# An attention loop whose two lanes run one score product apart, written two units to a body, with each small piece in a body of its own

## The chip, the core and the metric

The kernel runs on one core of a Trainium2 chip. The metric is the device time of one execution in microseconds (us): the median of several executions. An execution that the hardware profiler records gives the trace; times "in the trace" are counted from the start of its span.

## What is computed

Inputs are float32: q, k, v of 4 batches x 8 heads x 768 tokens x 64, 16 centroids for each head, and the matrices of a token mixing that follows. The reference, cut to its core:

```python
q_assign = np.argmax(np.einsum('bhsd,hcd->bhsc', q_n, c_n), axis=-1)
k_assign = np.argmax(np.einsum('bhsd,hcd->bhsc', k_n, c_n), axis=-1)
mask = q_assign[:, :, :, None] == k_assign[:, :, None, :]
scores = scale * np.matmul(q, k.transpose(0, 1, 3, 2))
scores = np.where(mask, scores, -1000000000.0)
scores = scores - np.max(scores, axis=-1, keepdims=True)
attn = np.exp(scores)
attn = attn / (np.sum(attn, axis=-1, keepdims=True) + 1e-09)
x = np.matmul(attn, v)                    # then (batch, token, 512)
...
theta = x @ w_theta
zr, zi = x * np.cos(theta), x * np.sin(theta)
y = np.einsum('ts,bsd->btd', w_tok_r, zr) + np.einsum('ts,bsd->btd', w_tok_i, zi)
u = x + y
return u + np.maximum(u @ w_ch, 0.0)
```

Every token goes to its nearest centroid, a query sees only the keys of its own cluster, and the result passes through a rotation, a mixing over the tokens and a small layer over the channels. The change touches the first part, the attention.

## The kernel before

**Tiling.** The 32 heads are taken in 16 pairs (`pi`). The two heads of a pair are the two lanes (`j`): lane 0 holds its 64 channels in partitions 0 to 63, lane 1 in 64 to 127. A matmul of one lane uses 64 rows of TensorE, and matmuls of both lanes that are next to each other in the program run at the same time. A pair is worked off in 12 units (`u`): 2 halves of the queries (`a`, 384 wide) by 6 blocks of 128 keys (`i`). There are 192 units (`NUT`), and one pass of the main loop (L784) is a body of two units, so a pair has six bodies.

**One unit.** Float32 values are kept as a rounded part and a rest (`hq`, `lq`, `hk`, `lk`). The scores of a lane are four matmuls into one PSUM bank (`score_products`, L455): hk with hq, hk with lq, lk with hq, and mk with mq. The last adds the mask: `mq` has a one at the row of the query's cluster and the negative maximum in row 32 of each lane, `mk` has a large negative number wherever a key is not in that cluster. ScalarE then exponentiates the bank (`exps`, L471), GpSimd adds the exponentials of three blocks to each other (`add_exps`, L482), VectorE adds the two sums that this leaves (`add_sums`, L486), and TensorE multiplies the exponentials by v (`weighted`, L543, the tile `av`). The maximum over the keys has to be known first. So in each body TensorE also computes, for a block of queries ten units ahead (`LEAD`), four products of each lane into a tile `m` of two banks (`max_products`, L410), which VectorE reduces (`max_of`, L430).

**PSUM.** There are two tiles of two banks (`m_tile`), three single banks (`bank`), and one bank for `av`. The score tiles `sc` and all small tiles take the three single banks in turn.

**Small pieces.** Besides its units, every pair needs on the way, two pairs ahead: its rows of q and k loaded (`load_raw`), their rounded parts (L390, L394), the centroid products `lg` (`logits`, L286, four matmuls), their transposition `lt` (`turn_logits`, L299, three), the maximum over 16 clusters, the comparison with it, the product with falling numbers and again the maximum (`find_max`, `first_of`: the first cluster that has the maximum, `rr`), the transposition of `rr` into `rt` (L350 or L354), its way through DRAM so that the cluster's number stands in 16 partitions (`rd`, then `clq` and `clk`, L359 and L364), and `mq` (two passes of ScalarE, L369 and L371) and `mk` (VectorE, L373) from these. For the maxima there is a transposition `mt` twice a pair (`shift_row`, L438), for the sums `sm` (L510) and their way through DRAM to `rb`, the multiply of `xt` (`normalise`), and for the second part of the kernel the unpacking of a piece of weights (`to_f32`: the operations that write `w`, and `hi`, `lo`).

**Order.** The order on each engine is that of the program; `in_order` fixes it. Tables give the unit at which a piece is written: `A_UNITS` for the ten steps of `assign`, `HI_UNITS` and `LO_UNITS` for the rounded parts, `W_UNITS` and `W_LAST` for the weights, `ADDS`, `SUMS`, `NORM` for the sums, `FIRST` for the first rotation of the second stage. `at_unit` collects them in `todo`, and `pieces(u)` writes those that are due, at three places of a body. In a body both lanes of unit u go in step; then unit u+1 of one lane at a time goes beside the m products of the other, with `av` between the two lanes:

```python
            both(score_products, u, exps)
...
            if ahead < NUT:
                scores_beside_max(u + 1, ahead, 0)
        pieces(u - 0.5)
        if 0 < u <= NUT:
            weighted(u - 2)
...
            weighted(u - 1)
...
        pieces(u)
```

When the maxima are done, ten units before the end, the m tiles take a part of the scores. SyncE issues nearly all transfers, in the order of the program.

Of the kernel before, what the change touches and what calls it, by code (L numbers as in the profile page):

```python
# [2 lines left out]

# [40 lines left out]
def kernel(  # L44
# [257 lines left out]
    def find_max(pi, ltv):  # L302
        mx = pe.tile([P, NG], F32, tag="mxl", name=f"mxl{pi}")
        nc.vector.tensor_reduce(out=mx, in_=ltv, op=ALU.max, axis=AX.X)
# [1 line left out]
        nc.vector.tensor_tensor(
            out=eq, in0=ltv, in1=mx.unsqueeze(2).broadcast_to([P, NG, C]), op=ALU.is_equal)
        return eq

    def first_of(pi, eq):  # L310
        nc.vector.tensor_tensor(out=eq, in0=eq, in1=wb, op=ALU.mult)
# [19 lines left out]
    def assign(pi):  # L331
# [15 lines left out]
        if "mt" in st.get(pi - 2, {}):  # L347
            mt = st[pi - 2].pop("mt")
            rt = mt[0:NG, P:2 * P]
            nc.tensor.transpose(out=rt, in_=rr, identity=identf)  # L350
# [11 lines left out]
        for n, x in enumerate("qk"):  # L362
            for j in range(2):
                nc.sync.dma_start(  # L364
                    out=cl[x][64 * j:64 * j + C], in_=rv[2 * n + j:2 * n + j + 1].broadcast_to([C, S]))
# [68 lines left out]
    def shift_row(pi, a):  # L434
# [5 lines left out]
        if a == 1 and 0 < pi < NPAIR - 2:  # L440

            s["mt"] = mt
        else:
            shift_out(pi, a, mt)
# [22 lines left out]
    def exps(u, j):  # L467
# [3 lines left out]
        last_exp[0] = nc.scalar.activation(out=s["at", a, i][:, j], in_=s["sc", j], func=AF.Exp, scale=SCALE)  # L471
# [627 lines left out]
```

## Time and profile before

| | |
|---|---|
| median of 3 runs | 786.07 us (784.77 to 786.43) |
| the profiled execution | 783.16 us, its span 781.4 us |
| TensorE clock granted | 1.00 |
| preparation, to the first unit | about 30 us of the span |
| attention, 16 pairs | from there to 441.8 us |
| token mixing | 441.8 us to the end |
| VectorE, ScalarE, GpSimd busy in the attention | 382.6, 265.9 and 370.7 of 411.3 us |

A time of the trace is a moment of the profiled execution or a duration; that execution was 2.9 us shorter than the median, so differences are worked out inside it. In the views a line such as `211.32 0.44 PE L408 MATMUL sc<-hq,hk` is start, length, engine, source line, operation, and the tile written with the tiles read. PE is TensorE, PEld its weight loads, DVE VectorE, ACT ScalarE, POOL GpSimd, SPq the queue of SyncE. A matmul of 384 columns is shown with 0.33 us, though the next pair of matmuls starts 0.17 us after it, since they are pipelined.

### The profile page before, as it was taken

The page shows a single profiled execution, that of the slowest core. Times are in us where ns is not written, and L with a number is a line of the kernel's source. Part 1 is how long each engine was busy: PE and PEld are TensorE (multiplying, and loading weights), DVE is VectorE, ACT ScalarE, POOL GpSimd, SP SyncE. Part 2 cuts the span into 40 slices and gives each one's busy share as a digit, 9 for nine tenths or more (in the row PEclk, how much of TensorE's full clock was granted, in tenths as well). Part 3 has the DMA queues.
Part 4 walks back from the last instruction along what each step waited for, and adds up shares of the span by engine and source line. Part 5 has one row for each costly group of instructions (what it writes and reads, how often), then busy time and mean ns, then how long its engine had stood idle before and what let it go on. Part 6 is the DMA issues. An engine that isn't in the chain of part 4 may idle for free.

```text
span 781.4 us, 14422 instructions
## 1 busy us (share of the span) xinstructions
PE 773.2 (99%) x5592; PEld 573.0 (73%) x5592; DVE 567.8 (73%) x689; ACT 388.2 (50%) x780; POOL 500.6 (64%) x289
## 2 busy tenths in 40 slices
PE   9999999999999999999999999999999999999998
PEld 6666565566666666566665588898889988899998
DVE  6789999999999999999989587844344444533322
ACT  3565757576767676767556455432333132503310
POOL 4568888989999999988987667561225112422231
PEclk9999999999999999999999999999999999999999
DMA  4113324432443244425354377124101411120001
GB/s 143 42 60 101 113 63 127 134 100 85 145 134 113 73 144 134 133 69 168 114 203 131 85 219 198 20 58 145 28 15 28 163 27 28 17 92 15 1 21 61
DMA packets 81708, 73.24 MB, mean 94 GB/s; under 512 B 59544, under 2 KB 65512, under 8 KB 81256
## 3 DMA queue, kind: packets, MB, share of 16 engines
q1 hardware_dynamic: 81634, 72.32, 31.2%
q8 instruction: 44, 0.72, 0.4%
q14 instruction: 24, 0.20, 0.1%
q10 hardware_dynamic: 6, 0.00, 0.0%
HBM read 56.89 MB, written 15.31 MB: 92 GB/s over the span
## 4 chain that ended last, share of the span: by engine, by line
PE 92%; DVE 4%; DMA 1%; issue 1%; SPq 1%; ACT 1%; POOL 0%; DVEq 0%
PE y L967 26%; PE sc L408 25%; PE av L543 15%; PE tp L643 7%; PE cy L990 5%; PE m L408 4%; PE cp L990 3%; PE lg L286 1%; PE sm L510 1%; PE y L990 1%; PE lt L299 1%; DVE acc L486 1%; DVE mk L373 1%; PE mt L438 1%; DVE nm L430 1%
## 5 line engine op out<-in xcount | busy, mean ns | idle before, releaser
L471 ACT ACTIVATE at<-sc 128x384 f32<-128x384 f32 x384 | 173.7, 495 | 97.6 <-PE m L408 57.5
L430 DVE TENSOR_REDUCE nm<-m 128x1 f32<-128x768 f32 x192 | 179.8, 946 | 21.0 <-PE m L408 19.9
L482 POOL TENSOR_TENSOR acc<-at,at 128x768 f32<-128x768 f32 x64 | 129.1, 2016 | 34.8 <-ACT at L471 34.8
L408 PE MATMUL m<-hk,hq 64*128 64x384 f32 x384 | 147.7, 385 | 0.8 <-DVE nm L430 0.6
L543 PE MATMUL av<-at,vt 128*64 128x384 f32 x768 | 145.3, 499 | 0.2 <-ACT xt L558 0.2
L918 POOL TENSOR_TENSOR zlc<-ab,zhc 128x512 fp32r<-128x512 f32 x24 | 32.9, 1371 | 162.7 <-ACT zhc L916 162.7
L482 POOL TENSOR_TENSOR acc<-acc,at 128x768 f32<-128x768 f32 x64 | 131.8, 2060 | 7.9 <-ACT at L471 5.7
L408 PE MATMUL m<-mk,mq 64*128 64x384 f32 x384 | 128.1, 334 | 0.0
L408 PE MATMUL sc<-hq,hk 64*128 64x384 f32 x384 | 117.7, 390 | 1.1 <-ACT at L471 0.9
L408 PEld LDWEIGHTS sc<-hq,hk 64*128 64x128 f32 x384 | 56.1, 183 | 61.8 <-issue 24.9
L408 PE MATMUL sc<-lq,hk 64*128 64x384 f32 x384 | 98.3, 335 | 0.0
L408 PE MATMUL sc<-mq,mk 64*128 64x384 f32 x384 | 97.8, 334 | 0.0
L408 PE MATMUL sc<-hq,lk 64*128 64x384 f32 x384 | 97.6, 333 | 0.0
L543 PEld LDWEIGHTS av<-at,vt 128*64 128x64 f32 x768 | 46.5, 136 | 58.6 <-issue 53.7
L408 PEld LDWEIGHTS m<-hk,hq 64*128 64x128 f32 x384 | 70.5, 183 | 3.3 <-DVE nm L430 2.6
L408 PEld LDWEIGHTS m<-mk,mq 64*128 64x128 f32 x384 | 71.1, 185 | 0.2 <-DVE mk L715 0.2
L649 DVE TENSOR_SCALAR kk<-tp 128x512 int32<-128x512 f32 x24 | 16.4, 685 | 73.2 <-PE tp L643 73.2
L486 DVE TENSOR_TENSOR acc<-acc,acc 128x768 f32<-128x768 f32 x30 | 69.0, 2302 | 0.0
L616 ACT CAST xh<-xT 128x512 fp32r<-128x512 f32 x23 | 14.3, 621 | 99.3 <-PE tp L643 99.3
L981 POOL TENSOR_TENSOR ul<-xT,uh 128x384 fp32r<-128x384 f32 (+1 forms) x36 | 33.5, 964 | 35.5 <-ACT uh L980 33.8
L408 PEld LDWEIGHTS sc<-mq,mk 64*128 64x128 f32 x384 | 55.3, 184 | 0.0
L408 PEld LDWEIGHTS sc<-hq,lk 64*128 64x128 f32 x384 | 55.2, 184 | 0.0
(174 smaller groups left out, 1716.3 us busy)
## 6 DMA issues: line engine op xcount, KB each, us to landing
vt<-in_v_dram SPq DMA_DIRECT2D x16, 384.0 KB
rb<-sd SPq DMA_DIRECT2D x32, 192.0 KB
xT_d<-xt SPq DMA_DIRECT2D x16, 384.0 KB
xb<-xT_d SPq DMA_DIRECT2D x96, 64.0 KB
rawq<-in_qT_dram SPq DMA_DIRECT2D x15, 384.0 KB
rawk<-in_kT_dram SPq DMA_DIRECT2D x15, 384.0 KB
w<-in_wrT_dram SPq DMA_DIRECT2D x6, 768.0 KB
xT<-xT_d SPq DMA_DIRECT2D x3, 1536.0 KB
```

What stands on the lines that cost most here:

```text
L408: nc.tensor.matmul(out, lhsT=stat[r, cols], rhs=mov[r, over], start=start, stop=stop)
L430: nc.vector.tensor_reduce(out=s["nm", a][:, j, i // 2:i // 2 + 1], in_=s["m", j][:, :, 0:HS], op=ALU.max, axis=AX.XY, negate=True)
L471: last_exp[0] = nc.scalar.activation(out=s["at", a, i][:, j], in_=s["sc", j], func=AF.Exp, scale=SCALE)
L482: last_acc[0] = nc.gpsimd.tensor_tensor(out=s["acc", a, x], in0=prev, in1=at, op=ALU.add)
L486: nc.vector.tensor_tensor(out=s["acc", a, 0], in0=s["acc", a, 0], in1=s["acc", a, 1], op=ALU.add)
L543: nc.tensor.matmul(s["av"][64 * j:64 * j + 64], lhsT=s["vt"][:, i, j, :], rhs=s["at", a, i][:, j], start=(i == 0), stop=(i == NT - 1))
L643: nc.tensor.matmul(tp, lhsT=xx[:, c, :], rhs=w_th[c][k], start=(n == 0), stop=(n == 3 * NCT - 1))
L649: nc.vector.tensor_scalar_mul(kk, tp, INV_2PI)
L918: nc.gpsimd.tensor_tensor(out=zl, in0=tr, in1=zh.bitcast(F32), op=ALU.subtract)
L967: last_mix[0] = nc.tensor.matmul(y_at(b, d, c0, c1), lhsT=zz[:, d * P:(d + 1) * P], rhs=ww[:, c0:c1], start=first and lead, stop=last, ski ...
L981: nc.gpsimd.tensor_tensor(out=ul[:, d, :], in0=x, in1=uh[:, d, :].bitcast(F32), op=ALU.subtract)
L990: nc.tensor.matmul(cp, lhsT=w_c[d][k][:, e * P:(e + 1) * P], rhs=uu[:, d, :], start=(n == 0), stop=(n == 3 * NCT - 1), skip_group_check=True)
```

## The change

**The lanes.** A body is written as one piece, after `av` and the pieces. Lane 1 is one product out of step with lane 0: where lane 0 stops a score tile, lane 1 has three of its four products done, or the other way round (`both_lanes`, and `begun` for three products that a body starts for the next one). The same matmuls are issued, in another order.

**The small pieces.** The tables are retuned: at most one of mt, lt, rt, sm and lg stands in a body, nearly always behind `av`. `lt` and `rt` take a single bank each. Before, `lt` had half of an m tile, and `rt` mostly shared the bank of a `mt`. The multiply of `xt`, the load of v, the loads of raw rows and the steps of the weights move to other units.

**The keys' mask.** `clk` is no longer one run of 768 numbers for a partition but three runs of 256 with four numbers of padding. Its loads get the same form, and so does the write of `mk`.

**The logit comparison.** `lt == maximum` is written back to PSUM in float32, and the product with the falling numbers is read from there and written as bfloat16. Before, the comparison wrote bfloat16 to SBUF, and the product read and wrote it there.

```diff
-NORM = (13, 16)
+NORM = (12, 15)
-ADDS = (8, 13)
+ADDS = (6.5, 14)
...
-    cl = {n: pe.tile([P, S], F32, name=f"cl{n}") for n in "qk"}
+    clk = pe.tile([P, 3, S // 3 + 4], F32, name="clk")
+    cl = dict(q=pe.tile([P, S], F32, name="clq"), k=clk[:, :, 0:S // 3])
...
-        lt = (m_tile(f"lt{pi}")[:, 0] if pi > 1 else bank(f"lt{pi}"))[:, 0:HS]
+        lt = bank(f"lt{pi}")[:, 0:HS]
...
+        nc.vector.tensor_tensor(
+            out=ltv, in0=ltv, in1=mx.unsqueeze(2).broadcast_to([P, NG, C]), op=ALU.is_equal)
         eq = pe.tile([P, NG, C], BF16, tag="eq", name=f"eq{pi}")
-        nc.vector.tensor_tensor(
-            out=eq, in0=ltv, in1=mx.unsqueeze(2).broadcast_to([P, NG, C]), op=ALU.is_equal)
+        nc.vector.tensor_tensor(out=eq, in0=ltv, in1=wb, op=ALU.mult)
         return eq
...
     def first_of(pi, eq):
-        nc.vector.tensor_tensor(out=eq, in0=eq, in1=wb, op=ALU.mult)
...
-        if "mt" in st.get(pi - 2, {}):
-            mt = st[pi - 2].pop("mt")
-            rt = mt[0:NG, P:2 * P]
-            nc.tensor.transpose(out=rt, in_=rr, identity=identf)
-            shift_out(pi - 2, 1, mt)
-        else:
-            rt = bank(f"rt{pi}")[0:NG, 0:P]
-            nc.tensor.transpose(out=rt, in_=rr, identity=identf)
+        rt = bank(f"rt{pi}")[0:NG, 0:P]
+        nc.tensor.transpose(out=rt, in_=rr, identity=identf)
...
+                row = rv[2 * n + j:2 * n + j + 1].broadcast_to([C, S])
                 nc.sync.dma_start(
                     out=cl[x][64 * j:64 * j + C],
+                    in_=(row if x == "q" else row.rearrange("c (a b) -> c a b", a=3)))
...
-    A_UNITS = (-9, -4, -2, -1, 2, 2, 3, 6, 7, 7.9)
+    A_UNITS = (-6, -1.5, 0, 1, 6, 6, 7, 9.5, 11.5, 10)
...
-            at_unit(u - NU + 7, load_v, pi)
+            at_unit(u - NU + 4.5, load_v, pi)
...
+    def both_lanes(p0, p1):
+
+        for x in zip_longest(p0, p1):
+            interleave(*([y] for y in x if y))
+
+    u, begun = 0, products(0, 0)
+    interleave(begun[:3])
...
+            a0, a1 = begun[3:], products(u, 1)
+            m = [max_products(ahead, j) for j in range(2)] if ahead < NUT else None
+            both_lanes(a0, a1[:1])
+            exps(u, 0)
+            if m:
+                both_lanes(m[0][:3], a1[1:])
+                exps(u, 1)
+                add_exps(u)
+                both_lanes(m[0][3:], m[1][:1])
+                max_of(ahead, 0)
+                b0 = products(u + 1, 0)
+                both_lanes(b0[:3], m[1][1:])
+                max_of(ahead, 1)
+                b1 = products(u + 1, 1)
...
+            both_lanes(b0[3:], b1[:1])
+            exps(u + 1, 0)
...
+            begun = products(u + 2, 0)
+            both_lanes(begun[:3], b1[1:])
+            exps(u + 1, 1)
             add_exps(u + 1)
```

HI_UNITS and LO_UNITS go to 3.0, 5.0 and 5.5, 7, the steps in W_UNITS move by up to 2.5 units, those in W_LAST (the last pieces of weights) by up to 11, and those in FIRST (the first rotation) by up to 1.5; the score tiles of the last bodies still take m tiles, one for each lane.

Where the instructions stand shows at three places. First TensorE, one body in the middle of the attention. In a name such as `sc86_0` 86 is the unit and 0 the lane; the number behind it counts tiles. Before:

```order
L408 MATMUL sc86_0_2999<-hq_1_145,hk_1_147 128x384
L408 MATMUL sc86_1_3000<-hq_1_145,hk_1_147 128x384
L408 MATMUL sc86_0_2999<-lq_1_146,hk_1_147 128x384
L408 MATMUL sc86_1_3000<-lq_1_146,hk_1_147 128x384
L408 MATMUL sc86_0_2999<-hq_1_145,lk_1_148 128x384
L408 MATMUL sc86_1_3000<-hq_1_145,lk_1_148 128x384
L408 MATMUL sc86_0_2999<-mq_1_149,mk_1_150 128x384
L408 MATMUL sc86_1_3000<-mq_1_149,mk_1_150 128x384
L408 MATMUL sc87_0_3013<-hq_1_145,hk_1_147 128x384
L408 MATMUL m96_1_3015<-hk_2_156,hq_2_154 128x384
```

And after the change, around the boundary of two bodies with lg (for pair 9) and lt in it:

```order
L406 MATMUL sc83_1_2927<-hq_0_163,lk_0_166 128x384
L406 MATMUL sc84_0_2932<-hq_1_145,lk_1_148 128x384
L406 MATMUL sc83_1_2927<-mq_0_167,mk_0_168 128x384
L288 MATMUL lg9_2941<-rawq9_2784,cb_188 32x384
L288 MATMUL lg9_2941<-rawk9_2786,cb_188 32x384
L288 MATMUL lg9_2941<-rawq9_2784,cb_188 32x384
L288 MATMUL lg9_2941<-rawk9_2786,cb_188 32x384
L537 MATMUL av78_2836<-at82_2880,vt6_2406 64x384 x2
L537 MATMUL av78_2836<-at83_2918,vt6_2406 64x384 x2
L301 MATMUL lt9_2956<-identf_66,lgs9_2946 128x2x4x16 x3
L406 MATMUL sc84_0_2932<-mq_1_149,mk_1_150 128x384
L406 MATMUL sc84_1_2965<-hq_1_145,hk_1_147 128x384
```

The two tiles of unit 86 stopped in one slot before; now lane 0 of unit 84 has its last product beside the first one of lane 1, and three of its products stand ahead of av. lt stands between them and takes a bank of its own.

Second VectorE, from lt to the third step of the weights (`w`, L144 to L153 before, L145 to L154 now; `acc` is L486 before and L480 now). Before:

```order
L304 TENSOR_REDUCE mxl_4345<-lt_4341 128x24
L306 TENSOR_TENSOR eq_4347<-lt_4341,mxl_4345 128x384
L430 TENSOR_REDUCE nm_4253<-m_0_4350 128x1
L311 TENSOR_TENSOR eq_4347<-eq_4347,wc 128x384
L313 TENSOR_REDUCE rr_4363<-eq_4347 128x24
L430 TENSOR_REDUCE nm_4253<-m_1_4380 128x1
L430 TENSOR_REDUCE nm_4253<-m_0_4398 128x1
L486 TENSOR_TENSOR acc_4231<-acc_4231,acc_4319 128x768
L430 TENSOR_REDUCE nm_4430<-m_1_4431 128x1
L144 TENSOR_SCALAR w_4290<-w_4290 128x768
L430 TENSOR_REDUCE nm_4430<-m_0_4462 128x1
L147 TENSOR_SCALAR w_4290<-w_4290 128x768
```

And now:

```order
L371 TENSOR_SCALAR mk_168<-clk,mcl,mbi 128x768
L306 TENSOR_REDUCE mxl_4380<-lt_4376 128x24
L307 TENSOR_TENSOR lt_4376<-lt_4376,mxl_4380 128x384
L310 TENSOR_TENSOR eq_4383<-lt_4376,wc 128x384
L428 TENSOR_REDUCE nm_4270<-m_0_4386 128x1
L428 TENSOR_REDUCE nm_4270<-m_1_4387 128x1
L315 TENSOR_REDUCE rr_4425<-eq_4383 128x24
L480 TENSOR_TENSOR acc_4246<-acc_4246,acc_4333 128x768
L145 TENSOR_SCALAR w_4187<-w_4187 128x768
L428 TENSOR_REDUCE nm_4441<-m_0_4442 128x1
L428 TENSOR_REDUCE nm_4441<-m_1_4443 128x1
L148 TENSOR_SCALAR w_4187<-w_4187 128x768
```

Maxima (`nm`) and other operations took turns one by one; now the two maxima of a body follow each other, and two or three other operations stand between two such pairs.

Third the queue of SyncE around the row loads of clq and clk. Before, and then now:

```order
L359 DMA rd_3395<-ri_3393 24x128
L364 DMA clq<-rd_3395 16x768 x2
L364 DMA clk<-rd_3395 16x768 x2
L277 DMA rawq_3415<-in_qT_dram 128x768
L277 DMA rawk_3417<-in_kT_dram 128x768
```

```order
L355 DMA rd_3492<-ri_3490 24x128
L279 DMA rawq_3494<-in_qT_dram 128x768
L279 DMA rawk_3496<-in_kT_dram 128x768
L361 DMA clq<-rd_3492 16x768 x2
L361 DMA clk<-rd_3492 16x3x256 x2
```

The row loads stand behind the loads of the raw rows of a later pair, and those of clk have three pieces to a row. On ScalarE the two passes of mq, which had two other operations between them, follow each other.

More of the change, by code (lines that the diff above doesn't have):

```diff
@@ L373, in assign @@
         nc.vector.tensor_scalar(
-            out=st[pi]["mk"], in0=cl["k"], scalar1=mcl, scalar2=mbi, op0=ALU.not_equal, op1=ALU.mult)
+            out=st[pi]["mk"].rearrange("p (a b) -> p a b", a=3), in0=cl["k"], scalar1=mcl, scalar2=mbi, op0=ALU.not_equal, op1=ALU.mult)
     st = {}
@@ L439, in shift_row @@
             out=mt[0:NT, 0:P], in_=s["nm", a].rearrange("p j t -> p (j t)"), identity=identf)
[L440 to L444, printed above, removed]
+        shift_out(pi, a, mt)
     def shift_out(pi, a, mt):
@@ L460, in score_products @@
             s["at", a, i] = p3.tile([P, 2, HS], F32, tag="at", name=f"at{u}", bufs=NAT)
-        sc = banks[:, j] if banks else ps.tile([P, 512], F32, tag="bank", name=f"sc{u}_{j}")
-        sc = s["sc", j] = sc[:, 0:HS]
+        sc = banks[:, j] if banks is not None else ps.tile([P, 512], F32, tag="bank", name=f"sc{u}_{j}")
+        sc = s["sc", u, j] = sc[:, 0:HS]
         k, q = slice(i * P, (i + 1) * P), slice(a * HS, (a + 1) * HS)
@@ L774 @@
         stages([u + NU + k for k in SUMS], sums(pi))
[L775 removed]
+        stages([u + NU + k for k in NORM], normalise(pi))
     for x, gen in enumerate(early_weights()):
@@ L791, in pieces @@
                     fn(*a)
-        if 0 <= u < NUT:
-            both(score_products, u, exps)
-            if u == 0:
-                for j in range(2):
-                    interleave(max_products(ahead - 2, j))
-                    max_of(ahead - 2, j)
-                for n, x in ((1, "mk"), (0, "mq")):
-                    nc.scalar.activation(
-                        out=st[1][x], in_=turn_one_hot(1, n), func=AF.Identity,
-                        **(dict(scale=BIG, bias=mbi) if n else {}))
-                nc.gpsimd.memset(cl["q"], -100.0)
-            add_exps(u)
-            if ahead < NUT:
-                scores_beside_max(u + 1, ahead, 0)
         pieces(u - 0.5)
@@ L812 @@
             weighted(u - 1)
-            if ahead >= NUT:
-                weighted_out(u - 1)
+            weighted_out(u - 1)
         pieces(u)
         if 0 <= u < NUT:
-            if ahead < NUT:
-                scores_beside_max(u + 1, ahead, 1)
-            else:
-                both(score_products, u + 1, exps, *([m_tile(f"sc{u + 1}")] if u < NUT - 6 else []))
+            if u == 0:
+                both(max_products, ahead - 2, max_of)
+            a0, a1 = begun[3:], products(u, 1)
[12 more added lines that the diff above has]
+                b1 = products(u + 1, 1)
+            else:
+                b0, b1 = (score_products(u + 1, j, m_tile(f"sc{u + 1}_{j}") if u < NUT - 6 else None) for j in range(2))
+                both_lanes(b0[:3], a1[1:])
+                exps(u, 1)
+                add_exps(u)
+            both_lanes(b0[3:], b1[:1])
+            exps(u + 1, 0)
+            if u == 0:
+                for n, x in ((1, "mk"), (0, "mq")):
+                    nc.scalar.activation(
+                        out=st[1][x], in_=turn_one_hot(1, n), func=AF.Identity,
+                        **(dict(scale=BIG, bias=mbi) if n else {}))
+                nc.gpsimd.memset(cl["q"], -100.0)
+            begun = products(u + 2, 0)
+            both_lanes(begun[:3], b1[1:])
+            exps(u + 1, 1)
             add_exps(u + 1)
-        if 0 < u and ahead < NUT:
-            weighted_out(u - 1)
         pieces(u + 1)
```

21 lines of the change are left out of this document (11 added, 10 removed).

## The prediction

> **What bounds the kernel now.** I read the page first, for the engine that ends last.
>
> ```profile
> span 781.4 us, 14422 instructions
> PE 773.2 (99%) x5592; PEld 573.0 (73%) x5592; DVE 567.8 (73%) x689; ACT 388.2 (50%) x780; POOL 500.6 (64%) x289
> PEclk9999999999999999999999999999999999999999
> PE 92%; DVE 4%; DMA 1%; issue 1%; SPq 1%; ACT 1%; POOL 0%; DVEq 0%
> ```
>
> TensorE is busy 99% of the span at full clock, and 92% of the chain that ended last is its own. So time can only come out of how its matmuls are spaced, or be lost where it is made to wait. The busy share hides small waits, since a waiting matmul counts as a long one. The second view is therefore the table by stretches, cut where the same work repeats (every 12 units, one pair of heads).
>
> ```profile
> 95.06:174.59 79.53, 78.91 (x644) 48.07 (x642) 78.20 (x73) 51.56 (x112) 71.78 (x36) 1.00 0.34 102
> 174.59:382.34 207.75, 207.75 (x1715) 126.88 (x1713) 197.08 (x192) 139.39 (x295) 199.60 (x95) 1.00 0.38 122
> 382.34:441.79 59.45, 57.69 (x439) 34.51 (x437) 50.41 (x48) 33.76 (x76) 46.84 (x24) 1.00 0.42 135
> ```
>
> The columns are length, then busy time of PE, PEld, DVE, ACT and POOL. Eight pairs take 207.75 us, 25.97 each, TensorE never idle, but VectorE busy 95% and GpSimd 96%: two more engines are almost full. Three earlier pairs take 26.51 each, with VectorE at 98%, and in the end of the attention TensorE is idle for 1.76. The third view is TensorE's timeline over one body of the loop (two units) with nothing else in it.
>
> ```profile
> 211.32 0.44 PE L408 MATMUL sc<-hq,hk 64*128 64x384 f32 x1
> ...
> 211.61 0.33 PE L408 MATMUL sc<-lq,hk 64*128 64x384 f32 x1
> ...
> 211.96 0.33 PE L408 MATMUL sc<-mq,mk 64*128 64x384 f32 x1
> ...
> 212.48 0.33 PE L408 MATMUL sc<-hq,lk 64*128 64x384 f32 x2
> 212.65 0.34 PE L408 MATMUL sc<-mq,mk 64*128 64x384 f32 x2
> 212.87 0.44 PE L408 MATMUL sc<-hq,hk 64*128 64x384 f32 x1
> ...
> 213.15 0.34 PE L408 MATMUL sc<-lq,hk 64*128 64x384 f32 x1
> ...
> 213.50 0.34 PE L408 MATMUL sc<-mq,mk 64*128 64x384 f32 x1
> ...
> 213.77 1.51 PE L543 MATMUL av<-at,vt 128*64 128x384 f32 x8
> 215.21 0.27 PE L438 MATMUL mt<-identf,nm 128*6 128x128 f32 x1
> 215.32 0.27 PE L350 MATMUL mt<-identf,rr 128*24 128x128 f32 x1
> 215.52 0.44 PE L408 MATMUL sc<-hq,hk 64*128 64x384 f32 x1
> ```
>
> Twelve slots of two matmuls (one of each lane) start 0.17 us apart, the first takes 0.29 (its weights could not be loaded ahead), the last is followed by av after 0.27, and av takes 1.44. But the ninth slot comes 0.22 after the eighth, and the tenth 0.28 after that: 0.16 more than the usual spacing. The waits say on whom:
>
> ```profile
> PEld sc L408 <- ACT at L471: 16.6, 76, 0.8
> ```
>
> and ScalarE's timeline says why:
>
> ```profile
> 212.33 0.49 ACT L471 ACTIVATE at<-sc 128x384 f32<-128x384 f32 x1 [0.32 <-PE m L408]
> ```
>
> The scores stopped at 211.96 are exponentiated from 212.33 to 212.82, and TensorE goes on at 212.87: a score bank comes back 0.91 us after its last product, while five slots are 5 x 0.17 = 0.87. There are three such banks, and this reuse comes in every body.
>
> **The change part by part, for one pair (six bodies).** A body without the wait is 3.89 - 0.16 = 3.73 us (211.32 to 215.21). With mt and rt 0.31, as above, and these from the chain of waits,
>
> ```profile
> 202.08 0.20 PE mt L438
> 202.28 0.78 PE lg L286 x8
> 206.96 0.48 PE lt L299 x3
> 219.47 0.78 PE sm L510 x8
> ```
>
> a pair is 6 x 3.73 + 0.31 + 0.20 + 0.78 + 0.48 + 0.78 = 24.9, and 25.97 is 1.0 above it. *Removed:* one lane now stops a slot ahead, and a bank is reused six slots after its stop (slot 4 to 10) or eight (1 to 9): 1.04 us or more against 0.91. So the 1.0 goes, where ScalarE is free to exponentiate at once. *Added,* by the order of the engines:
>
> rt gets a body of its own: 0.20 instead of 0.11, +0.1. lt now takes one of the three score banks, so in its body the reuse falls back to five slots (+0.16), and slot 10 waits until VectorE has read lt three times.
>
> ```profile
> 233.43 0.56 DVE L304 TENSOR_REDUCE mxl<-lt 128x24 f32<-128x384 f32 x1 [0.33 <-PE lt L299]
> 234.02 0.56 DVE L306 TENSOR_TENSOR eq<-lt,mxl 128x384 bf16<-128x384 f32 x1
> 235.36 1.39 DVE L311 TENSOR_TENSOR eq<-eq,wc 128x384 bf16<-128x384 bf16 x1
> ```
>
> Two of them follow each other by 0.59. No row shows a compare written to PSUM or a product read from it; the nearest rows, 0.56 with the operand in PSUM and 1.39 with all of it in SBUF, are the ends, and I take 0.56 for each. Then lt is free 0.1 + 0.59 + 0.59 + 0.56 = 1.84 after the first slot, and its bank is wanted at about 1.65 (0.29 + 8 x 0.17): +0.19. At 1.39 it would be +1.0. The Trainium skill, page "VectorE: DVE Perf Modes", section "The TRN2 errata", speaks against this part: it charges a PSUM source 120 fixed cycles and an SBUF one 58. By that, as an estimate from the page, the product costs 0.53 us from PSUM and 0.26 from packed bf16 in SBUF, and the pair would lose 0.3; the trace has 1.39 for the SBUF form, so the row decides.
>
> VectorE, then, gets back 1.39 - 0.56 = 0.83 there. Why its SBUF operation is slow shows against GpSimd, and the same rows price mk.
>
> ```profile
> 227.54 1.22 DVE L373 TENSOR_SCALAR mk<-clk,mcl,mbi 128x768 fp32r<-128x768 f32 x1
> 228.68 2.60 DVE L486 TENSOR_TENSOR acc<-acc,acc 128x768 f32<-128x768 f32 x1
> 231.21 0.94 DVE L430 TENSOR_REDUCE nm<-m 128x1 f32<-128x768 f32 x1
> ```
>
> ```profile
> 226.53 1.81 POOL L482 TENSOR_TENSOR acc<-acc,at 128x768 f32<-128x768 f32 x1
> 228.30 2.17 POOL L482 TENSOR_TENSOR acc<-at,at 128x768 f32<-128x768 f32 x1
> 230.55 2.42 POOL L482 TENSOR_TENSOR acc<-acc,at 128x768 f32<-128x768 f32 x1
> ```
>
> mk ends 0.42 after GpSimd's first add does, acc 0.81 after its second, and the add behind each is longer by about as much (2.17 and 2.42 against 1.81): they take turns, a whole operation each. From padded rows mk lies between 0.94 (the 768-element row that does not wait) and 1.22; I take 0.94, and 0.36 back for GpSimd. Hidden either way: VectorE has 5% to spare. Row loads in three pieces have no row: between nothing and 0.44, one more issue like clk's below, and I take nothing, since mk follows some bodies later.
>
> ScalarE gets mq's two passes back to back, after row loads that now stand behind rawk in SP's queue; rawk waits for GpSimd's lq.
>
> ```profile
> 245.76 0.88 SPq L364 DMA_DIRECT2D clk<-rd  x2
> 247.46 0.35 SPq L277 DMA_DIRECT2D rawk<-in_kT_dram  x1
> ```
>
> ```profile
> 249.15 0.93 ACT L369 ACTIVATE mq<-clq,ncl 128x768 fp32r<-128x768 f32 x1
> 251.79 0.86 ACT L371 ACTIVATE mq<-mq 128x768 fp32r<-128x768 f32 x1
> ```
>
> Behind 0.93 + 0.86 stand the next body's exps, for which TensorE's slot 10 waits. The last exp starts 0.37 after slot 12 (2.38 after the first slot); mq runs from about 2.8 to 4.5, 0.8 into the next body of 3.73; an exp that starts up to 0.6 in is in time: +0.16. If the row loads land late, more: between 0 and 0.7, I take 0.25 for all.
>
> VectorE's pieces now come in bunches between two pairs of maxima: acc and w, then w and w. With turns as above the second of a bunch waits for a whole add. I find 0.1 lost (bounds 0 and 1.2, below).
>
> Sum for a pair: -1.0 + 0.1 + 0.35 + 0.25 + 0.1 = -0.2; thirteen such pairs -2.6. The three pairs of 26.51 lose 0.54 each at
>
> ```profile
> 128.61 0.44 PE L408 MATMUL sc<-hq,hk 64*128 64x384 f32 x1
> 129.08 0.44 PE L408 MATMUL m<-hk,hq 64*128 64x384 f32 x1
> ```
>
> where m waits behind lt's tile; lt leaves those tiles: -1.6. Of the 1.76 at the end, where the score tiles stay those of the m pool but the order is the new one, I take -1.0 (-1.8 to +2: the last weight pieces come up to eleven units later there, the first rotation up to 1.5). Loads of vt and the multiply of xt move by a body or less, with bodies to spare before their use: nothing. The second stage is unchanged. Together -5.2: the profiled execution's 783.16 us (span 781.4) would be 778.0. The runs' median, 786.07, lies 2.9 above that execution, so I forecast 786.1 - 5.2, about **781.0**, 776 to 784 for this case.
>
> **Rivals.** *Everything is hidden.* ScalarE in time, lt read early: 13 x (-1.0 + 0.1) - 2.6 = -14.3, about 771.8. For: the body has no other wait. Against: lt on three banks.
>
> *No net change.* mq is held by its row loads. If the transfer of rawk ends after ScalarE is free, mq and the exps behind it come 0.5 later, and the -0.2 a pair becomes +0.2: 13 x 0.2 - 2.6 = 0, 786.1. For: the queue order above. Against: in the trace the row loads are issued 3 us ahead of mq.
>
> *Slower.* VectorE's bunches decide. In the body after lt, VectorE issues acc about 4.0 us after lt's first slot. If GpSimd is then inside the pair's first add (to 5.7), acc ends at 6.5, w after one more add at 8.8, and with two maxima of 0.94 the second m tile is free at 10.7; it is wanted 0.7 into the body that begins at 8.8 (3.73 + 0.35 + 0.20, then 3.73 + 0.78), so TensorE waits 1.2. If GpSimd is still at the multiply before it, w passes one add earlier and the loss is 0.1. So it turns on one GpSimd operation of 1.8 us. Price: 13 x 1.1 = +14.3 on the forecast, 795. For it: GpSimd is 96% full, and the pieces are fewer and thicker. Against: its 199.60 is 24.95 a pair, without the turns of mk and eq some 24.5, against 25.8: 1.3 of slack. The Trainium skill, page "SBUF — State Buffer", section "SBUF: two separate sides", has the turns as a rule, an exclusive lock held "for the full instruction"; the trace's rows of mk and acc agree, and its result here is this rival.
>
> **How the numbers follow.** Forecast 0.45, all hidden 0.13, no net change 0.17, slower 0.25. Differences under 0.2% (1.6 us) can't be told from none. Faster is the first two, 0.58; same 0.17; slower 0.25. The range takes in most of the hidden case and of the slower one, 771 to 794, and leaves about 0.1 out at each end or less.
>
> **What would show it.** Right: in a plain body all spacings of slots 2 to 12 are 0.17, and the wait of sc's weight loads on ScalarE falls from 16.6 us; mk near 0.94 and the product near 0.56; pairs of 25.4 to 25.9. The slower case shows as m's weights waiting for VectorE's nm two bodies after lt; the no-change case as ScalarE waiting for the DMA of clq ahead of mq. Wrong altogether would be a lane that runs alone: slots longer than 0.17 because the two lanes no longer start together.

## The result, and the profile after

| | before | after |
|---|---|---|
| median of 4 runs each | 785.74 us | 808.24 us (804.74 to 810.61) |
| profiled execution, its span | 783.16, 781.4 us | 804.74, 803.0 us |
| ratio after to before | | 1.0288 (95% interval 1.0256 to 1.0320) |

The change makes the kernel 2.9% slower, 22.5 us, where 781.0 was forecast and 794 was the end of the range. The page of the changed kernel, the engines and the chain that ended last:

```profile
PE 779.1 (97%) x5592; PEld 580.4 (72%) x5592; DVE 506.9 (63%) x689; ACT 403.7 (50%) x780; POOL 476.0 (59%) x289
PE 78%; DMA 11%; ACT 5%; issue 3%; DVE 1%; SPq 1%; POOL 1%; ACTq 0%; POOLq 0%
PE y L980 25%; PE sc L406 13%; PE av L537 12%; PE tp L637 8%; DMA clq<-rd 6%; DMA rd<-ri 5%; PE m L406 5%; PE cy L1003 5%; PE cp L1003 3%; ACT at L465 2%; ACT mq L367 2%; PE sm L504 2%; PE lg L288 1%; PE y L1003 1%; PE lt L301 1%
```

VectorE and GpSimd have less to do than before (568 and 501 us there), TensorE's share of the chain falls from 92% to 78%, and two small transfers that are not among the chain's lines before now hold 11% of it: rd, 12 KB, and clq, two loads of 48 KB. The table by stretches, for the same 48 bodies that took 207.75 us before:

```profile
181.61:404.33 222.72, 211.75 (x1714) 131.06 (x1713) 165.32 (x193) 147.46 (x295) 183.89 (x95) 0.99 0.36 112
```

That is 15.0 us more for eight pairs, 27.84 a pair against 25.97, and TensorE is idle for 11 of them. First a body with nothing in it, on TensorE's timeline:

```profile
413.57 1.51 PE L537 MATMUL av<-at,vt 128*64 128x384 f32 x8
415.01 0.44 PE L406 MATMUL sc<-mq,mk 64*128 64x384 f32 x1
...
415.82 0.33 PE L406 MATMUL m<-hk,hq 64*128 64x384 f32 x1
415.99 0.33 PE L406 MATMUL sc<-hq,hk 64*128 64x384 f32 x1
...
416.51 0.51 PE L406 MATMUL sc<-hq,hk 64*128 64x384 f32 x2
417.30 0.54 PE L537 MATMUL av<-at,vt 128*64 128x384 f32 x2
```

It takes 3.73 us from av to av, as the prediction had it, and after the first slot every slot follows by 0.17. So the lanes do what was expected of them. Then the body at unit 10 of a pair (with lg at its end), which should take 3.73 + 0.78, and takes 6.58 here (212.92 to 219.51). TensorE and ScalarE in it:

```profile
215.89 0.34 PE L406 MATMUL sc<-mq,mk 64*128 64x384 f32 x1
217.62 0.82 PE L406 MATMUL sc<-hq,hk 64*128 64x384 f32 x2 [1.40 <-ACT at L465]
```

```profile
212.56 0.97 ACT L465 ACTIVATE at<-sc 128x384 f32<-128x384 f32 x2 [0.44 <-PE sc L406]
215.37 0.94 ACT L367 ACTIVATE mq<-clq,ncl 128x768 fp32r<-128x768 f32 x1 [1.85 <-DMA clq<-rd]
216.34 0.84 ACT L369 ACTIVATE mq<-mq 128x768 fp32r<-128x768 f32 x1
217.09 1.23 ACT L465 ACTIVATE at<-sc 128x384 f32<-128x384 f32 x3
```

ScalarE, free at 213.5, waits 1.85 us for clq; mq's two passes follow, and only then the exponentials whose banks TensorE needs. The waits say that this is the rule:

```profile
ACT mq L367 <- DMA clq<-rd: 22.2, 14, 2.8
```

14 pairs, 22.2 us. That this comes so near to the cost of the change is partly chance: the 14 bodies with mq take 25.8 us more than bodies without mq, the bodies behind two of them, at a lower clock, 2.5 more, and the rest of the attention gains 6.9. Why clq is late stands in SyncE's queue:

```profile
206.93 0.33 SPq L137 DMA_DIRECT2D w<-in_wrT_dram  x1
207.31 0.56 SPq L517 DMA_DIRECT2D sd<-se  x1
207.96 0.42 SPq L355 DMA_DIRECT2D rd<-ri  x1
208.43 0.34 SPq L279 DMA_DIRECT2D rawq<-in_qT_dram  x1
210.40 0.33 SPq L279 DMA_DIRECT2D rawk<-in_kT_dram  x1
212.87 0.81 SPq L361 DMA_DIRECT2D clq<-rd  x2
213.73 0.88 SPq L361 DMA_DIRECT2D clk<-rd  x2
```

and in the trace's records of the packets in that stretch (worked out from them: bytes, count, first and last start, end):

```
6144 x128  (w)                 207.90  210.58  210.82
 512 x24   (rd)                210.19  211.78  211.87
3072 x288  (rawq, rawk, clq)   210.24  214.58  214.91
1024 x96   (clk)               214.80  215.69  215.74
```

rd is issued at 207.96, but its packets start 2.2 us later, when the 768 KB of a weight piece, issued 1.03 us ahead of it, are nearly through, and the last two of them pass at 211.8, between those of rawq. SyncE issues clq when rd has landed, at 212.87 (it waits for that in 11 of the 14 pairs; in the others clq follows rawk at once), and clq's packets then pass with the last of rawk or right behind them. From the end of ri to mq it takes 8.2 us, where before it took 7.1 without a wait, and ScalarE now comes for it after 6.3.

### The profile page after: what moved, and what is told of

Read it like the earlier page. It is cut to its first block, busy times and chain, and to the rows that moved or that the text cites. A ratio compares the mean times of both kernels' runs of the same rounds, so it can differ in the third digit from the quotient of the medians.

```text
span 803.0 us, 14365 instructions
## 1 busy us (share of the span) xinstructions
PE 779.1 (97%) x5592; PEld 580.4 (72%) x5592; DVE 506.9 (63%) x689; ACT 403.7 (50%) x780; POOL 476.0 (59%) x289
## 4 chain that ended last, share of the span: by engine, by line
PE 78%; DMA 11%; ACT 5%; issue 3%; DVE 1%; SPq 1%; POOL 1%; ACTq 0%; POOLq 0%
PE y L980 25%; PE sc L406 13%; PE av L537 12%; PE tp L637 8%; DMA clq<-rd 6%; DMA rd<-ri 5%; PE m L406 5%; PE cy L1003 5%; PE cp L1003 3%; ACT at L465 2%; ACT mq L367 2%; PE sm L504 2%; PE lg L288 1%; PE y L1003 1%; PE lt L301 1%
## 5 line engine op out<-in xcount | busy, mean ns | idle before, releaser
L406 PE MATMUL sc<-hq,hk 64*128 64x384 f32 x384 | 132.4, 378 | 17.5 <-ACT at L465 16.1
L406 PE MATMUL sc<-mq,mk 64*128 64x384 f32 x384 | 137.7, 361 | 0.0
L476 POOL TENSOR_TENSOR acc<-acc,at 128x768 f32<-128x768 f32 x64 | 129.3, 2020 | 13.5 <-ACT at L465 10.7
L406 PE MATMUL m<-hk,hq 64*128 64x384 f32 x384 | 114.9, 337 | 1.5 <-DVE nm L428 1.5
L406 PE MATMUL m<-mk,mq 64*128 64x384 f32 x384 | 116.3, 340 | 0.0
L406 PE MATMUL sc<-lq,hk 64*128 64x384 f32 x384 | 114.6, 342 | 0.0
L406 PE MATMUL sc<-hq,lk 64*128 64x384 f32 x384 | 111.4, 334 | 0.0
L406 PEld LDWEIGHTS sc<-hq,hk 64*128 64x128 f32 x384 | 69.9, 183 | 34.7 <-ACT at L465 27.9
L406 PEld LDWEIGHTS sc<-mq,mk 64*128 64x128 f32 x384 | 70.6, 184 | 29.7 <-issue 24.3
L406 PEld LDWEIGHTS sc<-hq,lk 64*128 64x128 f32 x384 | 68.9, 184 | 0.0
L406 PEld LDWEIGHTS sc<-lq,hk 64*128 64x128 f32 x384 | 64.3, 185 | 0.0
```

Source lines behind the costliest of these rows:

```text
L406: nc.tensor.matmul(out, lhsT=stat[r, cols], rhs=mov[r, over], start=start, stop=stop)
L476: last_acc[0] = nc.gpsimd.tensor_tensor(out=s["acc", a, x], in0=prev, in1=at, op=ALU.add)
```

## The experiments

Thirteen kernels were run. The kernel before ran beside each, with a median of 783.0 to 783.1 us on the same chip; the ratio is to it. The changed kernel was measured ahead of these, beside a median of 785.74, so what a run gives back is worked out from its ratio and the 1.0288 of the change. A block is six bodies with the starts of av as its ends, counted from the first av, and its median is taken over blocks 2 to 13 of each trace (before 25.97, changed kernel 27.45).

| run | median us | ratio (95%) | block |
|---|---|---|---|
| e1_rows_first | 808.72 | 1.0328 (1.0297 to 1.0359) | 27.78 |
| e2_w_later | 799.03 | 1.0205 (1.0165 to 1.0246) | 26.91 |
| e3_clk_flat | 808.83 | 1.0323 (1.0278 to 1.0368) | 27.95 |
| e4_mq_late | 792.51 | 1.0118 (1.0103 to 1.0133) | 26.46 |
| e5_both | 783.57 | 1.0005 (0.9991 to 1.0018) | 25.86 |
| e6_both_w15 | 787.08 | 1.0057 (1.0041 to 1.0073) | 26.24 |
| e7_w15_sbuf | 788.11 | 1.0060 (1.0045 to 1.0074) | 26.43 |
| b2_mask_eq | 786.27 | 1.0037 (1.0024 to 1.0049) | 26.32 |
| e8_in_step | 805.18 | 1.0276 (1.0254 to 1.0299) | 26.93 |
| e9_w75 | 804.17 | 1.0245 (1.0221 to 1.0270) | 28.03 |
| e10_w75_abs13 | 800.51 | 1.0216 (1.0193 to 1.0240) | 27.37 |
| e11_abs13 | 781.58 | 0.9990 (0.9978 to 1.0002) | 25.82 |
| e12_abs13_w15 | 787.72 | 1.0064 (1.0051 to 1.0076) | 25.85 |

### What makes clq late

**e1_rows_first**

```diff
-    A_UNITS = (-6, -1.5, 0, 1, 6, 6, 7, 9.5, 11.5, 10)
+    A_UNITS = (-6, -1.5, 0, 1, 6, 6, 6, 9.5, 11.5, 10)
```

> The row loads of clq and clk are written one step earlier, so that they stand right behind the write of rd in SyncE's queue and ahead of rawq and rawk; nothing else moves. In the changed kernel ScalarE waits for clq in all 14 pairs, 22.2 us in all, and TensorE loses 1.5 to 3.0 us in the body that follows. Theory A (the queue order: clq is issued behind rawk, which waits for GpSimd, and its packets pass behind 768 KB of rawq and rawk): clq arrives 1.5 to 2 us earlier, ScalarE's wait falls from 22.2 to under 5 us, and the time falls by 15 to 22 us, to 786 to 793. Theory B (rd's packets pass behind the 768 KB of a weight piece issued just ahead of it, and the rows can't start before): the wait falls by less than half, the time stays above 797. Theory C (the three-piece rows of clk are what is slow): no change of clq, 808. Theory D (the two passes of mq on ScalarE, back to back, are the cost, whether or not the data is there): the wait goes, but TensorE still loses over 1 us a pair, 800 or more.

No gain. ScalarE's wait for clq falls only from 22.2 to 14.9 us, and one pair shows why in SyncE's queue:

```profile
202.18 0.33 SPq L137 DMA_DIRECT2D w<-in_wrT_dram  x1
202.57 0.56 SPq L517 DMA_DIRECT2D sd<-se  x1
203.22 0.61 SPq L355 DMA_DIRECT2D rd<-ri  x1
206.93 0.78 SPq L361 DMA_DIRECT2D clq<-rd  x2
```

clq is next in the queue behind rd, and is still issued 3.7 us after it: rd itself is behind the weight piece. Three early pairs bear that out: there the piece ahead of rd has 512 KB, ScalarE no longer waits for clq, and the body with lg takes 4.70, 4.70 and 5.16, where the changed kernel has 6.19, 6.01 and 7.21. That the time does not fall even by what ScalarE gains has a second reason. SyncE now stands on rd's landing for 38.2 us in all (11.8 in the changed kernel), and what is behind clq in the queue comes late: VectorE waits for sq, the sums that it reads back, for 63.4 us in all, where it waited 33.9 in the changed kernel.

**e2_w_later**

```diff
-    W_UNITS = (5.5, 11.0, 14, 15, 15, 17, 19.5)
+    W_UNITS = (8.5, 11.0, 14, 15, 15, 17, 19.5)
```

> The load of a weight piece (768 KB, a transfer of about 2.8 us) is written two bodies' steps later (unit 8.5 for 5.5), behind rd, rawq, rawk, clq and clk. Theory A (clq waits for rawk's issue and for rawq and rawk's packets): rd lands about 2 us earlier, but clq is still issued behind rawk; ScalarE's wait falls by less than half, the time stays above 797. Theory B (the weight piece ahead of rd is the delay): rd, and with it clq, lands 2 to 2.5 us earlier, the wait falls from 22.2 to under 5 us, the time falls to 785 to 793. Theories C and D: 800 or more.

6 to 7 us of the 22.5 come back. The wait falls to 14.1 us, but no further. SyncE in one pair:

```profile
202.37 0.33 SPq L355 DMA_DIRECT2D rd<-ri  x1
202.74 0.35 SPq L279 DMA_DIRECT2D rawq<-in_qT_dram  x1
205.74 0.33 SPq L279 DMA_DIRECT2D rawk<-in_kT_dram  x1
206.17 0.84 SPq L361 DMA_DIRECT2D clq<-rd  x2
```

Now rawk is in the way: SyncE stands 2.7 us on GpSimd's lq before it issues rawk, and clq is issued behind it, though rd has landed by then. Each of the two runs came out as the other theory had it: neither A nor B alone was right.

**e3_clk_flat**: clk as one run of 768 again, its loads and mk as before the change.

```diff
-    clk = pe.tile([P, 3, S // 3 + 4], F32, name="clk")
-    cl = dict(q=pe.tile([P, S], F32, name="clq"), k=clk[:, :, 0:S // 3])
+    cl = {n: pe.tile([P, S], F32, name=f"cl{n}") for n in "qk"}
```

> clk is one run of 768 for a partition again (loads and mk as before the change); all else stays. Theory C (three-piece rows slow the loads): 10 us or more faster. Theories A, B and D: clq is loaded ahead of clk and its time doesn't change, so TensorE's loss stays; mk on VectorE goes from 1.06 to 1.2 us and more and takes turns with GpSimd again, which VectorE at 63% hides: 806 to 811.

Same time as the changed kernel, the wait for clq 25.3 us: theory C is out. What it shows of mk is told below.

**e4_mq_late**

```diff
-    A_UNITS = (-6, -1.5, 0, 1, 6, 6, 7, 9.5, 11.5, 10)
+    A_UNITS = (-6, -1.5, 0, 1, 6, 6, 7, 11, 12.9, 13)
```

> The first pass of mq is written at the end of the body (unit 11 for 9.5), the second and mk at the end of the next one, so that ScalarE reaches clq about 4 us later and the two passes no longer follow each other; the queues stay as they are. Theories A and B (the data is late, whatever delays it): the wait of ScalarE for clq falls from 22.2 to under 2 us and the time falls by 20 to 28 us, to 780 to 788; the body with lg takes 4.5 to 4.8 us for 6.2. Theory C: the same here. Theory D: the passes cost TensorE wherever they stand, half of it stays: 795 or more. If only ScalarE's wait goes, and the body with lt still takes 4.7 (against 4.21 without a wait), that part belongs to lt in a score bank.

The wait is gone (0.6 us in all) and the body with lg takes 4.70 in place of 6.2, but only 13 us come back, and the time stays above the 780 to 788 that were expected. Nine of the twelve blocks take 26.2 to 27.6, nearly all of the excess in the body with sm (4.9 to 6.3 for 4.52). TensorE's weight loads, then VectorE and GpSimd ahead of that:

```profile
197.55 0.18 PEld L406 LDWEIGHTS m<-hk,hq 64*128 64x128 f32 x1 [1.26 <-DVE nm L428]
```

```profile
190.70 1.06 DVE L371 TENSOR_SCALAR mk<-clk,mcl,mbi 128x768 fp32r<-128x768 f32 x1
191.68 0.55 DVE L315 TENSOR_REDUCE rr<-eq 128x24 f32<-128x384 bf16 x1
192.14 2.40 DVE L480 TENSOR_TENSOR acc<-acc,acc 128x768 f32<-128x768 f32 x1
194.46 2.17 DVE L145 TENSOR_SCALAR w<-w 128x768 f32<-128x768 f32 x1
196.55 1.81 DVE L428 TENSOR_REDUCE nm<-m 128x1 f32<-128x768 f32 x2
```

```profile
191.86 1.85 POOL L476 TENSOR_TENSOR acc<-at,at 128x768 f32<-128x768 f32 x1
193.80 2.42 POOL L476 TENSOR_TENSOR acc<-acc,at 128x768 f32<-128x768 f32 x1
```

acc ends just after one add of GpSimd, w just after the next, and the maxima come 1.3 us late. This is the mechanism of the prediction's slower rival, in its place and near its price (1.2). But the run's own edit has a hand in it: it also moves mk, 1.06 us, to unit 13, into the same bunch. In e5 below, where mk keeps its place and ScalarE does not wait for clq either, the body with sm takes 4.52 to 4.73, and m waits for nm for 2.8 us in all, as in the changed kernel (10.7 here). That mk makes the difference is likely, but no run moves it alone.

**e5_both**: the edits of e1 and of e2 together, which restores the order of the queue before the change.

> Both moves at once: the row loads ahead of rawq and rawk, and the weight piece's load behind them, which is the order of the queue that the kernel before had. Each move alone left ScalarE waiting for clq (14.9 and 14.1 us of 22.2). Theory A+B (rd behind the weight piece, and clq behind rawk's issue and the raw rows: either alone is enough to be late): the wait falls under 2 us and the body with lg falls to 4.5 to 4.8 us; 14 x 1.84 = 26 us less than the change. What is late next, by the run with mq moved (m's weights waited 10.7 us for VectorE's maxima, 20 times): VectorE's bunch of acc and the first step of w, each behind a whole add of GpSimd, costs 0 to 1.4 us a pair. So 782 to 798 on the scale where the change has 808, ratio to the kernel before 1.00 to 1.015. Rival (the passes of mq themselves, 1.8 us of ScalarE ahead of the exponentials, hold TensorE even when clq is there): the body with lg still takes over 5.2 us.

The wait for clq is 0.7 us in all, and the time is back at that of the kernel before. SyncE and ScalarE in one pair:

```profile
249.92 0.33 SPq L355 DMA_DIRECT2D rd<-ri  x1
251.25 0.79 SPq L361 DMA_DIRECT2D clq<-rd  x2
...
256.03 0.36 SPq L137 DMA_DIRECT2D w<-in_wrT_dram  x1
```

```profile
255.25 0.97 ACT L465 ACTIVATE at<-sc 128x384 f32<-128x384 f32 x2 [0.44 <-PE sc L406]
256.11 0.93 ACT L367 ACTIVATE mq<-clq,ncl 128x768 fp32r<-128x768 f32 x1
257.07 0.85 ACT L369 ACTIVATE mq<-mq 128x768 fp32r<-128x768 f32 x1
```

clq is issued 1.3 us after rd, and mq follows the exponentials with nothing between. The body takes 4.70: the two passes themselves cost 0.17. So the 22 us are the order of SyncE's queue, and both faults have to go.

### What the parts are worth

**e8_in_step**: e5 with the lanes in step again, all else as there.

```diff
-            both_lanes(a0, a1[:1])
-            exps(u, 0)
...
+            both(score_products, u, exps)
+            add_exps(u)
+            if ahead < NUT:
+                scores_beside_max(u + 1, ahead, 0)
+                scores_beside_max(u + 1, ahead, 1)
```

> The run with both moves (its order of the queue, its tables, all pieces as there), but the lanes of a body in step again: both lanes of unit u, then unit u+1 lane by lane beside the m products, all of it behind av. If the lanes' step apart is what takes the standing wait for a score bank away: the wait of 0.16 is back in every body, the plain body 3.9 for 3.75, a pair 0.9 to 1.0 longer, 16 x 0.95 = 15 us slower than the run with both moves (ratio to the kernel before about 1.02). More than that is possible where av, now right behind the last score product, waits for its exponential. Rival (writing the body in one block, or the pieces, took the wait away, not the step between the lanes): within 3 us of the run with both moves.

The block is 26.93 against 25.86: 1.07 more, the plain body with mt 4.14 to 4.16 against 3.94 to 3.97, with a slot that starts 0.27 after the one ahead, as in the kernel before:

```profile
208.42 0.34 PE L406 MATMUL sc<-mq,mk 64*128 64x384 f32 x1
208.69 0.44 PE L406 MATMUL sc<-hq,hk 64*128 64x384 f32 x1
```

So the step between the lanes is what takes the standing wait away, at the forecast size (the three products started ahead of av belong to it and go with it in this run). The run is 22 us slower than e5, more than 16 x 1.07 = 17: two of its blocks (30.95 and 29.79) lost more.

**b2_mask_eq**: the kernel before with the padded clk and the comparison in PSUM, the parts called "The keys' mask" and "The logit comparison" above; lt stays in an m tile.

> The kernel before with the two edits on VectorE's operations alone (clk in padded rows with mk from it, and the comparison in PSUM with the product from there; lt stays in half an m tile, the lanes and tables stay as they were). VectorE's mk falls from 1.22 to 1.06 us and the product from 1.39 to 0.56, and GpSimd's adds beside them get 0.4 to 0.8 us shorter. If TensorE in the kernel before is held by nothing but the standing wait for a score bank: no change, ratio 0.998 to 1.002. If the waits of m for VectorE in the first pairs (3 x 0.54) and at the end (1.76) come from a full VectorE: 1 to 3 us faster. Against both: m's tile is held longer by lt, since the product now reads it too (up to 0.6 a pair): up to 8 us slower.

0.4% slower. VectorE's operations get as short as expected, but lt's body takes 4.78 to 4.80 for 4.45: the product holds lt's tile 0.56 longer, and m's weights wait for that tile. The block is 26.32, with the three blocks of 26.5 at the start gone. So relief of VectorE alone bought nothing, and the comparison in PSUM needs a tile that nobody waits for.

**e6_both_w15** and **e7_w15_sbuf** are e5 with VectorE's first step of w at unit 15 (14 in W_UNITS becomes 15), and e7 also has the comparison and product in SBUF:

```diff
-        nc.vector.tensor_tensor(
-            out=ltv, in0=ltv, in1=mx.unsqueeze(2).broadcast_to([P, NG, C]), op=ALU.is_equal)
         eq = pe.tile([P, NG, C], BF16, tag="eq", name=f"eq{pi}")
-        nc.vector.tensor_tensor(out=eq, in0=ltv, in1=wb, op=ALU.mult)
+        nc.vector.tensor_tensor(
+            out=eq, in0=ltv, in1=mx.unsqueeze(2).broadcast_to([P, NG, C]), op=ALU.is_equal)
+        nc.vector.tensor_tensor(out=eq, in0=eq, in1=wb, op=ALU.mult)
```

> As the run with both moves, and the first step of a weight piece on VectorE (the min/max that writes w) at unit 15 instead of 14: then rr and acc stand alone between two pairs of maxima, and the three steps of w between the next two. Theory E (the bunch: acc and w each wait for one whole add of GpSimd, so the second m tile comes back late): m's waits for nm fall under 3 us in all, and the time is 4 to 12 us below the run with both moves, at or below the kernel before. Rival F (VectorE waits for the sums or for GpSimd's adds that are late anyway, wherever w stands): no change to the run with both moves, or the same wait one body later.

> As the run before it, with the logit comparison written to bfloat16 in SBUF and the product made there, as before the change, right behind the comparison; lt stays in a score bank. The body with lt took 4.71 us in the changed kernel, 0.5 above 3.73 + 0.48; 0.29 of it is the slot that waits for lt's bank, which VectorE reads three times. If PSUM is the better place: the bank comes back 0.56 earlier, which takes up to 0.3 off that body, but the product takes turns with GpSimd and takes 0.6 to 1.9 us, so VectorE's maxima come later: 0 to 5 us slower. If the bank decides: lt's body 4.4 to 4.5 us, 13 x 0.25 = 3 us faster. If both are hidden: within 1 us.

e6 is 3.5 us slower than e5. In five pairs ScalarE waits for w ahead of its exponentials, 6.0 us in all, but e5 has about as much of that (5.6 in three pairs). Most of the difference lies in two blocks (28.4 each, where e5 has 25.8 and 27.0): there the three steps of w take turns with GpSimd's adds (1.21, 2.07 and 2.48 us), m's weights wait 1.0 and mt's 1.9. In e7 lt's body falls from 4.71 to 4.38, so 0.33 of it was lt's bank; but the product now takes 0.36 to 1.89 us, mt's weights wait for VectorE's maxima for 16.8 us in all, and the sum is no better than e6.

### What is left

**e9_w75** moves w's load in e5 from 8.5 to 7.5, **e10_w75_abs13** also abs from 11 to 13.

```diff
-    W_UNITS = (8.5, 11.0, 14, 15, 15, 17, 19.5)
+    W_UNITS = (7.5, 11.0, 14, 15, 15, 17, 19.5)
```

> The run with both moves, with the weight piece's load one unit earlier (7.5 for 8.5), right behind rawk. With both moves three pairs were 0.6 to 1.2 us above the 25.8 of the others, each in the body with lt, where ScalarE waited for the weight piece (up to 1.64 us) ahead of the exponentials. If the late weight piece is their cause: they go to 25.8, the time falls by 2 to 4 us, to a ratio of 0.996 to 0.999 to the kernel before. If the piece now passes ahead of something else in the queue (sq, or the rows of the next step): no gain, ratio 1.00 or above.

> As the run before it, and ScalarE's first step of the weight piece (abs, 0.92 us) at unit 13 for 11, behind the exponentials of the body with lt instead of ahead of them. That body took 4.71 us; its slot 5 starts 0.04 late and a later slot 0.24 late, the first behind ScalarE (lgs 0.48, abs 0.92, xt 0.48 stand ahead of its exponentials), the second behind lt's bank. If ScalarE counts there: 0.05 to 0.2 us a pair, 1 to 3 us faster than the run before it. If only lt's bank counts: within 0.5 us. Against: abs one body later lets VectorE's first step of w start later, behind acc; m may wait for nm then: up to 5 us slower.

e9 is 20 us slower than e5, for a place ahead of sq and two small loads in the queue. SyncE and VectorE of e9:

```profile
212.58 0.33 SPq L137 DMA_DIRECT2D w<-in_wrT_dram  x1
212.97 0.42 SPq L520 DMA_DIRECT2D sq<-sd  x1
```

```profile
218.90 0.23 DVE L522 RECIPROCAL sq<-sq 128x12 f32<-128x12 f32 x1 [6.47 <-DMA sq<-sd]
219.04 1.75 DVE L428 TENSOR_REDUCE nm<-m 128x1 f32<-128x768 f32 x2
```

sq, 6 KB, now stands behind the weight piece, VectorE waits 6.5 us for it ahead of a reciprocal of 0.23, and the maxima and lt's comparison stand behind that: 63.3 us in 13 pairs, where e5 has 23.8. It is the same fault on another engine. A part of the 20 us is the granted clock, which in four places of the attention stands at 0.5 for 3.4 us. e10 takes 3.7 us less than e9, a little more than the 1 to 3 expected, and keeps the fault (57.9 us).

**e11_abs13** is e5 with abs at 13 for 11 (nothing moves in the queue), **e12_abs13_w15** also has the first step of w at 15.

> The run with both moves (weight piece loaded at unit 8.5 again, behind sq), with ScalarE's abs of the piece at unit 13 for 11: no queue changes, but ScalarE reaches the piece about 3 us later, behind the exponentials of the body with lt. If the three pairs that took 26.4 to 27.0 instead of 25.8 were ScalarE waiting for the piece ahead of its exponentials: they go to 25.8, and lt's body loses its first small wait; 3 to 6 us faster than the run with both moves, ratio to the kernel before 0.992 to 0.997. If those pairs come from VectorE and GpSimd taking turns: no gain, 0.999 to 1.002. Against: the piece's first step on VectorE follows abs sooner, and a late piece would now hold VectorE and with it m: slower than before, 1.003 or more.

> As the run beside it, with VectorE's first step of the piece at unit 15 for 14, so that abs has a body more and acc no longer stands next to it. If m's waits for VectorE come from that bunch: 0.5 to 3 us faster than the run beside it. If the piece's last step, and with it the next piece's load, comes later by it: 1 to 4 us slower, as it was 3.5 us slower without the move of abs.

e11 takes ScalarE's wait for w away, and with 781.58 us it is the fastest of all, but its ratio, 0.9978 to 1.0002, does not part it from the kernel before, nor from e5. Eight of its twelve blocks take 25.78 to 25.91; of the others (26.31 to 26.76) three have 5.01 to 5.34 in place of 4.53 in the body with sm, where m waits for the bunch of acc and w, and in the fourth VectorE waits 3.65 us for sq. So both theories were partly right: the pairs that were long in e5 are cured, and others lose to VectorE's turns. In e12 the blocks are as short, but for three (28.72, 28.70 and 27.08); three steps of w in one bunch are no better than acc and w.

## Why the prediction was wrong

**The term that failed** is mq: "If the row loads land late, more: between 0 and 0.7, I take 0.25 for all." It measured 1.8 a pair. The fourteen bodies with mq take 25.8 us more than 3.75, or 4.53 with lg. The prediction had seen that the rows stand behind rawk and that rawk waits for GpSimd. It did not look at what the queue holds ahead of rd (a weight piece, whose load the retuned table brings from unit 8 to 5.5, next to rd), and its bound of 0.7 rests on no row. Of the rival "no net change" the mechanism was right (mq held by its rows) and the size was not: it had 0.5 later, and e1, e2 and e5 show two delays, of 2.2 us (rd's packets) and 2.7 us (SyncE at rawk) in the pairs shown, each enough to make ScalarE wait. The sign that the prediction named for this rival, ScalarE waiting for the DMA of clq ahead of mq, is what the trace shows. Its argument against, that the rows were issued 3 us ahead of mq, came from a queue whose order the change undoes.

**The lanes** were right: 1.0 a pair forecast, 1.07 by e8, the plain body 3.73. The wait of sc's weight loads on ScalarE, which was to fall from 16.6 us, is 27.9 in the changed kernel, behind mq, and 10.7 in e5.

**lt in a score bank** was forecast at 0.35 and measured 0.48 (4.71 against 3.75 + 0.48); by e7 0.33 of it is the bank, 0.15 is left without it. **rt** costs its 0.2, and mq's passes with data in time 0.17.

**The product** takes 0.56: the choice between 0.56 and 1.39, which no row decided, came out. **mk** takes 1.06, inside 0.94 to 1.22, where 0.94 was chosen. Both are hidden, as forecast, and VectorE has 63% to do.

**The end of the attention** was forecast at -1.0 and is -0.5 in e5: from the same body to the last av 59.5 us before, 59.0 there. The last two blocks gain 2.0 (24.64 and 25.1 before, 23.98 and 23.76 in e5), but the five bodies behind them lose 1.2, and 0.3 of the gain lies ahead of that stretch.

With the queue's order restored the sum for an undisturbed pair holds: seven of the twelve blocks of e5 take 25.8, 0.17 less than 25.97 where -0.2 was forecast. That it comes so close is partly luck: lt costs 0.13 more than forecast, mq's passes 0.08 and VectorE's bunches 0.1 less. The total doesn't hold: -5.2 was forecast, and e5 is no faster than the kernel before. Its other five blocks lose 3.3 us, 2.8 of it in three pairs where ScalarE waits for w; the stretch from the start to block 2 takes 1.4 more (57.6 for 56.2), for which the prediction had no term. The kernel before has no such pairs: its blocks from 174.6 us on are all within 0.02 of each other.

**The slower rival** has a mechanism that the rows of e4 show, near its price, but with mk in the bunch as well. In e5 it costs 0.2 at most in a pair, in three pairs of e11 0.5 to 0.8. So for this change the forecast's 0.1 was nearer than the rival's 1.2, and the wait for clq was not what hid it.

## What to carry to other kernels

A small transfer costs what stands ahead of it in its queue: when steps move, list for each short load that an engine waits for which large transfers are now issued shortly before it, and which wait the issuing engine meets on the way. Two delays that are each sufficient hide each other, so undoing one part at a time can show no gain; undo them together before a theory is dropped. And a move that cures one wait moves its neighbours too: e1 made sq late, e4 put mk into a bunch, e9 put a large load ahead of sq. Name what is late next before the gain is counted.

## What was not expected of the hardware

**The granted clock falls after short waits.** In the changed kernel two of the fourteen stalls are followed by some 3 us at nearly half the clock. The table by stretches, the second and fourth row right behind the stall:

```profile
128.77:135.98 7.21, 5.81 (x43) 2.89 (x41) 3.58 (x5) 4.01 (x8) 6.40 (x5) 0.91 0.31 80
135.98:138.50 2.52, 2.52 (x13) 0.83 (x10) 0.00 (x0) 1.05 (x2) 2.35 (x2) 0.58 0.13 29
295.36:302.20 6.84, 5.30 (x42) 2.87 (x40) 3.58 (x5) 4.02 (x8) 6.84 (x5) 0.98 0.27 81
302.20:305.60 3.40, 3.40 (x16) 1.23 (x13) 0.00 (x0) 1.76 (x3) 3.32 (x3) 0.54 0.20 64
```

The first number behind GpSimd's is the clock: 0.58 and 0.54, and av takes 2.46 and 2.76 us in place of 1.44, though TensorE had been idle for only 1.4 and 1.5 us. Other stalls as long or longer (1.40 us up to 217.6, 2.36 up to 330.5) left the clock at 1.00. So a stall can cost twice its length, and which ones do, no run here shows. The changed kernel's runs fit that: they spread over 6 us, with a mean granted clock of 0.996 in the shortest and 0.992 in the longest, where those of the kernel before spread over 2. The Trainium skill, page "TensorE: Matmul & The Clock Gate", section "What's actually happening", gives about 3.4 us of idleness for this; here less than half of that did it.

**Padded rows make mk slower alone and steadier in company.** With clk in three runs mk takes 1.06 us every time; as one run, in e3, these are the shortest, middle and longest:

```profile
L370 DVE TENSOR_SCALAR mk<-clk,mcl,mbi x14: 672/851/1991, 53.3 to 421.8; 128x768 fp32r<-128x768 f32 x14
```

The product does the same: 557 ns always with its source in PSUM, 357 to 1887 from SBUF in e7. The Trainium skill, page "SBUF — State Buffer", section "SBUF: two separate sides", has an exclusive lock between the two engines; the rows agree, and show forms of an operation that never wait for it.
